# A state-space convolution with a gated MLP: all side jobs of the kernel generation get new places, and the ring buffers new letters

## The chip, the cores and the metric

One core of a Trainium2 chip. The metric is the device time of one execution in microseconds, median of three runs.

## What is computed

`A_u` (called x below) is 2048 positions of 640 channels. A vector `c` gives six modulation rows (scale, shift and gate, twice) by one product with `w_mod`. The first half is a state-space convolution with 192 complex states for each channel: a kernel of 2048 taps is generated and convolved with the modulated input. The second half is a bilinear gated MLP of width 1536. Cut to what matters:

```python
mod = (silu(c) @ w_mod).reshape(1, 6, 1, 640)
sa, ca, ga, sb, cb, gb = mod rows
h = layernorm(x) * (1 + ca) + sa
logdA = exp(log_dt)[:, None] * (A_re + 1j * A_im)
K = einsum("dn,dnl,dn->dl", C, exp(logdA[:, :, None] * l), dt * B).real
y = irfft(rfft(pad(h)) * rfft(pad(K)))[..., :2048] + h * Dskip
x = x + ga * y
h = layernorm(x) * (1 + cb) + sb
out = x + gb * (((h @ w_gate) * (h @ w_up)) @ w_down)
```

## The kernel before

**Kernel generation.** The 640 channels are five groups of 128 (`db` 0 to 4), each generated in eight blocks, 40 blocks (`NK`) in all. The loop at L1325 takes three steps `t` for a block `n`. In a block POOL makes three outer products (`outer`, L716): phases `Pha` or `Phb` (int32), then `EQ`, then `EP`, for the block that follows. ACT takes sines and absolute values of the phases (`tra`, `trb`, `ab`, all through the helper at L230). DVE multiplies them by EQ and EP (`QtA` and `QtB` L771 and L772, `PtA` L777, `PtB` L797). PE contracts the results over the states into a PSUM tile `kg` (L812, L827), and ACT copies it out as `Kt`. EQ and EP have two buffers each, so an EQ can be made only when the QtB two blocks back has read its buffer. For each group the tables of these products come from *seeds* (`u_seeds`): a chain over DVE (to L625), ACT (exponentials, an arctangent), PE (L532 to L534) and DVE (L650, L651). Its last results release POOL's L656, which is followed by the integer tables LH (L699 to L701, L680) and the float table LQ (L710, L711, L680). After the 40 blocks the loop goes on for 24 steps; then comes the GLU.

**Side jobs.** Everything else of the first half runs beside the blocks as generators, each cut into a few parts: `mod_l` loads the modulation weights from `w_mod` (L356), `u_modr` makes a row of the modulation from them (L363) and ACT copies it (tiles TVa, TVb); `u_stats` loads x (L471) and takes its statistics, `u_hm` normalises it on ACT (128 x 640 activations on tiles gha, ghb, f16a and others); `u_k` is the first transform stage of the kernel (L849 on PE, a copy f16b or f16a on ACT); `u_pre` the forward transform of the input (L861 to L884); `u_g` loads a quarter of its spectrum (L910) and carries out the second stage (L894), whose result ACT copies; `u_c` multiplies the spectra (L894 on PE, L935 to L940 on DVE), goes back one stage (L950), copies W on ACT and stores it to DRAM (L955); `u_d` loads it again with x (L963, L965), finishes on PE (L971), adds on DVE (L975 or L978) and stores the row (L979). For the MLP raw weights are loaded (L1004) and split in two parts (`split_g`, L1026), and the *head* normalises the first rows (L1139 and on, L1171, L1206 on PE).

**What sets the order.** Scheduling is manual: each engine carries out its instructions in the order in which the Python code emits them. Nearly all DMAs are issued by SP, in that order too, so a DMA that waits holds back those behind it. A table `SCHED` has for each part of each job a number. `at` files a generator under `v // 10`, a half-step of the loop, and `due` runs those of a half-step in the order of their numbers, so the numbers decide both where a part stands among the blocks and which job comes first. Negative numbers place a part in the seeds of group 0, ahead of the loop. Which letter of a ring of buffers an allocation gets (three PSUM banks `psf`, two each of `TV`, `W`, `tr`, `xs`, three of `gh` and `hf`) stands in the strings of `SLOT`, one letter for each allocation in order of emission; a letter given again is a wait for the tile's former readers.

```python
def at(ts, g, *a):
    it = g(*a)
    for v in ts:
        jobs.setdefault(v // 10, []).append((v, it))
def due(x):
    for _, g in sorted(jobs.pop(x, []), key=lambda j: j[0]):
        next(g, None)
```

## Time and profile before

| | us |
|---|---|
| median of 3 runs | 981.17 (979.21 to 988.58) |
| the profiled execution, its own time | 987.31 |
| its span in the profile | 985.5 |
| PE busy | 892.4 (91%) |
| DVE busy | 717.3 (73%) |
| ACT busy | 579.4 (59%) |
| POOL busy | 513.1 (52%) |
| mean granted TensorE clock | 0.955 |

The shares are means over two halves with different limits: kernel generation to about 437 us, a tail to about 527 us, and the GLU from there. So the prediction reads stretches apart. A row of the timeline is: start, duration, engine, line, operation, output <- inputs, shapes, count, and in brackets the idle time ahead of it with what ended it. A tile's name is cut to its letters (gha, ghb and ghc are one ring).

### The profile page before, as it was taken

How to read it: one execution, taken by the hardware profiler on the slowest of the kernel's cores; microseconds unless marked ns; L12 is line 12 of the kernel's file. 1: busy time of each engine (PE TensorE's matmuls, PEld its weight loads, DVE VectorE, ACT ScalarE, POOL GpSimd, SP SyncE). 2: the span in 40 equal slices, each digit the busy share in tenths (PEclk: the TensorE clock that was granted, in tenths of full speed). 3: DMA queues.
4: the chain of work that ended last, by engine and by line, in shares of the span. 5: the costliest groups of instructions: out<-in, count | busy, mean ns of one | idle time of the engine just before them, and what ended most of it. 6: DMA issues, size and time to landing. Idle time of an engine off the chain costs nothing.

```text
span 985.5 us, 26662 instructions
## 1 busy us (share of the span) xinstructions
PE 892.4 (91%) x11134; PEld 725.6 (74%) x11134; DVE 717.3 (73%) x1297; ACT 579.4 (59%) x1076; POOL 513.1 (52%) x400
## 2 busy tenths in 40 slices
PE   4767898899789888999879999999999999999998
PEld 3565656686476667677636888889999788888997
DVE  8798569888978888794867755557676656578952
ACT  4869989986878797873336433334455443435430
POOL 5988899799779979970030254440113132322110
PEclk9977789899989889999999999999999999999999
DMA  7746664555255434658695666733564576758875
GB/s 260 257 151 212 213 198 137 175 174 173 77 154 175 146 114 116 192 166 269 208 257 189 230 202 188 240 110 132 176 224 129 192 234 220 233 168 293 243 239 187
DMA packets 158816, 188.53 MB, mean 191 GB/s; under 512 B 9828, under 2 KB 128360, under 8 KB 157544
## 3 DMA queue, kind: packets, MB, share of 16 engines
q1 hardware_dynamic: 149480, 155.51, 49.1%
q0 software_dynamic: 4752, 21.63, 7.6%
q10 hardware_dynamic: 4464, 9.70, 2.6%
q8 instruction: 87, 1.43, 0.6%
q14 instruction: 33, 0.27, 0.1%
HBM read 124.22 MB, written 62.59 MB: 190 GB/s over the span
## 4 chain that ended last, share of the span: by engine, by line
PE 56%; ACT 14%; DVE 13%; issue 10%; POOL 4%; DMA 3%; SPq 0%; POOLq 0%; ACTq 0%; DVEq 0%
PE pa L1078 18%; PE psg L1078 9%; PE pa L1502 7%; PE kg L812 2%; PE kg L827 2%; PE psfc L894 2%; PE psfb L894 2%; PE psfc L950 2%; ACT trb L230 2%; ACT L230 2%; PE psfa L894 1%; ACT tra L230 1%; DVE QtA L772 1%; DVE QtA L771 1%; PE psfc L873 1%
## 5 line engine op out<-in xcount | busy, mean ns | idle before, releaser
L1055 POOL TENSOR_TENSOR tf<-wur,wgb 128x256 f32<-128x256 f32 x23 | 17.4, 755 | 243.0 <-DVE wtl L1026 196.5
L716 POOL TENSOR_TENSOR EQ<-LQ,RH 128x1536 f32<-128x1536 f32 x40 | 124.2, 3106 | 8.3 <-DVE QtB L772 8.1
L1026 DVE TENSOR_TENSOR wtl<-tf,wth 128x256 fp32r<-128x256 f32 (+1 forms) x72 | 37.3, 520 | 58.6 <-ACT wth L230 58.4
L716 POOL TENSOR_TENSOR Phb<-LH,DH 128x1536 int32<-128x1536 int32 x20 | 62.3, 3114 | 13.2 <-ACT tra L230 13.2
L716 POOL TENSOR_TENSOR EP<-LP,RH 128x768 f32<-128x768 f32 x40 | 66.1, 1653 | 0.0
L716 POOL TENSOR_TENSOR Pha<-LH,DH 128x1536 int32<-128x1536 int32 (+1 forms) x21 | 62.5, 2974 | 1.9 <-ACT trb L230 1.6
L1502 PE MATMUL pa<-wsg,sh 128*128 128x384 f32 (+1 forms) x304 | 57.3, 307 | 0.0
L827 PE MATMUL kg<-QtB,PtB 64*32 64x64 f32 x2560 | 49.3, 232 | 7.1 <-DVE QtB L772 7.1
L827 PEld LDWEIGHTS kg<-QtB,PtB 64*32 64x32 f32 x2560 | 42.8, 117 | 17.1 <-DVE QtB L772 8.5
L1541 POOL DMA_DIRECT2D wsg<-wdc x21 | 11.1, 531 | 66.5 <-PE pa L1554 35.5
L1502 PEld LDWEIGHTS pa<-wsg,sh 128*128 128x128 f32 x304 | 45.1, 188 | 0.0
L1026 DVE TENSOR_TENSOR wsg<-wga,wsg 128x640 fp32r<-128x640 f32 x36 | 33.8, 946 | 13.2 <-ACT wsg L230 13.2
L230 ACT ACTIVATE sh<-a 128x512 fp32r<-128x512 f32 x55 | 33.3, 624 | 13.9 <-PE psg L1554 6.2
L1026 DVE TENSOR_TENSOR sl<-a,sh 128x512 fp32r<-128x512 f32 x55 | 38.0, 710 | 3.9 <-ACT sh L230 3.9
L230 ACT ACTIVATE wsg<-wga 128x640 fp32r<-128x640 f32 x36 | 26.1, 730 | 24.8 <-PE pa L1502 12.1
L1078 PE MATMUL pa<-hh,wsg 128*128 128x512 f32 x150 | 39.9, 392 | 0.0
L771 DVE TENSOR_TENSOR QtA<-tra,EQ 128x1024 f32<-128x1024 f32 x20 | 24.4, 1221 | 18.1 <-PE kg L812 8.7
L1148 POOL TENSOR_SCALAR hfa<-xb,hr,hr 128x128 f32<-128x128 f32 x4 | 2.3, 577 | 67.0 <-DVE hr L285 67.0
L230 ACT ACTIVATE s<-pa 128x512 f32<-128x512 f32 x12 | 7.2, 599 | 49.1 <-PE pa L1078 49.1
L230 ACT ACTIVATE a<-pa 128x512 f32<-128x512 f32 x12 | 7.2, 597 | 48.4 <-PE pa L1078 48.4
L230 ACT ACTIVATE wth<-tf 128x256 fp32r<-128x256 f32 (+1 forms) x72 | 32.5, 482 | 4.6 <-DVE tf L1056 1.8
L1078 PE MATMUL pa<-sh,wth 128*128 128x512 f32 x110 | 34.0, 390 | 0.4 <-ACT a L230 0.4
(640 smaller groups left out, 3125.4 us busy)
## 6 DMA issues: line engine op xcount, KB each, us to landing
wsg<-wdc POOLq DMA_DIRECT2D x21, 640.0 KB, 4.8
wgb<-B_w_gate SPq DMA_DIRECT2D x24, 320.0 KB, 4.7
wur<-B_w_up SPq DMA_DIRECT2D x24, 320.0 KB, 5.7
wsd<-wsg SPq DMA_DIRECT2D x12, 640.0 KB, 4.2
wga<-wdg SPq DMA_DIRECT2D x12, 640.0 KB, 4.0
wsg<-wsd POOLq DMA_DIRECT2D x12, 640.0 KB, 4.9
wdc<-xb SPq DMA_DIRECT2D x21, 320.0 KB, 3.4
TVb<-WD SPq DMA_DIRECT2D x22, 256.0 KB, 3.4
```

Of the source, the lines that this page charges most:

```text
L230: return S.activation(o, i, f, **kw)
L716: G.tensor_tensor(o.rearrange("p x (h l) -> p x h l", l=8), lo.unsqueeze(2).to_broadcast([P, rows, nh, 8]), hi.rearrange("p h x -> p x h") ...
L771: return [lambda: V.tensor_tensor(Qt[:, :, :, 0:32], tr[:, :, :, ::-1], e[:, :, 0:32].unsqueeze(1).to_broadcast([P, 2, R, 32]), op=OP.mult ...
L812: PE.matmul(kg[j * 32 : j * 32 + 32, dd, :], PtA[:, c, dl * 4 + j, :], QtA[:, c, dl * 4 + j, :], start=dd == 0 and c == 0, stop=False, til ...
L827: PE.matmul(kg[j * 32 : j * 32 + 32, dd, :], PtB[lo : lo + 64, c, r, :], QtB[lo : lo + 64, c, r, :], start=False, stop=dd == 7 and c == 1, ...
L894: PE.matmul(r[c][par * 64 : par * 64 + 64, i, :], t_tw[:, k0 + k, c, :], src[:, k, :], start=True, stop=True, tile_position=(0, par * 64))
L950: PE.matmul(r[par][:, i], t_ti[lo : lo + 64, qd * 4 + i, c, :], x[lo : lo + 64, c, i, :], start=c == 0, stop=c == 1, tile_position=(lo, 0))
L1026: V.tensor_tensor(lo, v, hi, op=OP.subtract)
L1055: E.tensor_tensor(t[:, 0:2], u[:, 0:2], g[:, 0:2], op=OP.subtract)
L1078: PE.matmul(ps, w[a][:, k], x[b][:, l], start=first and n == 0 and m == 0, stop=n == 2 and m == len(ks) - 1, skip_group_check=True)
L1502: PE.matmul(AC[tb][t][c], x[:, ts], w[:, cs], start=st, stop=f == NF - 1 and n == 2 and (c == 0 or t % 2 == 1))
L1541: G.dma_start(WD[q], wdc[:, q // 3, q % 3])
```

## The change

All numbers of `SCHED` are new, and all strings of `SLOT` but `Ph`, `PtA`, `tr` and `f16` (which move in the listing only). No other code differs; the two tables take five more lines, so what was L716 is L721 in the changed kernel, and so on. Each engine has the same instructions in the same numbers; their order differs. A few lines of the tables:

```diff
 SCHED = dict(
-    ml=(-885, -929, -989),
-    mr=(((98, 154), (90, 130)), ((-884, 78), (-877, 73)), ((-885, -881), (-889, 132))),
+    ml=(-880, -916, -945),
+    mr=(((84, 129), (83, 116)), ((-876, 68), (-865, 68)), ((-884, -866), (-881, 7))),
...
-        (338, 577, 594, 672, 676, 688, 718, 745, 812, 816, 825, 855, 872, 872),
+        (500, 538, 549, 670, 678, 691, 732, 742, 805, 811, 826, 845, 859, 866),
...
-        ((2816, 2835, 2861), (2847, 2876, 2876), (2862, 2877, 2878), (2876, 2879, 2879)),
+        ((2776, 2797, 2829), (2804, 2829, 2837), (2780, 2819, 2834), (2844, 2871, 2873)),
...
-    low=((145, 411, 641, 885, 1122, 1398, 1592, 1847, 2073), (209, 434, 680, 929, 1150, 1398, 1612, 1868, 2112)),
+    low=((157, 412, 659, 886, 1134, 1375, 1599, 1842, 2071), (199, 425, 699, 916, 1176, 1367, 1611, 1845, 2116)),
...
-        ((2376, 2550, 2610), (2354, 2464, 2495), (2390, 2442, 2446), (2382, 2455, 2492)),
+        ((2420, 2582, 2583), (2433, 2488, 2511), (2342, 2445, 2481), (2424, 2465, 2485)),
...
 SLOT = dict(
-    gh="abcaacbabcbcbcbacbacabccabcacbabcabc",
+    gh="abcbbcaacacaacabbacbbcaacbacbacbacab",
```

(`ml`, `mr`: the modulation's loads and rows; the third is the seeds of group 1; then `d` of group 4; `low`: LH and LQ tables, first the row for `tab_ph`, then for `tab_eq`; then `g` of group 4.)

Three places show what this does. The first is the start, on SP: loads of x (L471) around the first load of modulation weights, before and then now.

```order
L471 DMA gha<-A_u 128x640
L471 DMA ghb<-A_u 128x640
L356 DMA t_tw<-w_mod 128x5x640
L471 DMA f16a<-A_u 128x640
L471 DMA Wa<-A_u 128x640
L471 DMA ghc<-A_u 128x640
```

```order
L476 DMA gha<-A_u 128x640
L476 DMA f16a<-A_u 128x640 x3
L476 DMA ghb<-A_u 128x640
L476 DMA f16a<-A_u 128x640
L361 DMA t_tw<-w_mod 128x5x640
L476 DMA ghc<-A_u 128x640
```

Two loads of x stood ahead of the weights, and six do now. On PE, the same place: the first modulation rows, behind the seeds' last products. Before, then now:

```order
L534 MATMUL tra<-ct,pta 64x8x8
L363 MATMUL psfb<-t_tw,sil 128x256 x5
L363 MATMUL psfa<-t_tw,sil 128x384 x5
L363 MATMUL psfa<-t_ti,sil 128x384 x5
L363 MATMUL psfc<-t_ti,sil 128x256 x5
```

```order
L539 MATMUL tra<-ct,pta 64x8x8
L368 MATMUL psfb<-t_tw,sil 128x384 x5
L368 MATMUL psfa<-t_tw,sil 128x256 x5
L368 MATMUL psfc<-t_ti,sil 128x384 x5
L368 MATMUL psfb<-t_ti,sil 128x256 x5
```

The 384 wide group of each pair has gone ahead of the 256 wide one (the third and fourth row already stood so). ACT's copy of the 384 wide row stands ahead of the first sines, as before; the copy of the other one stands behind the first pair of them.

The second place is DVE at the end of block 5, with the seeds of group 1. Before, from block 5's PtB on:

```order
L797 TENSOR_TENSOR PtB<-tra,EP_145 128x512
L771 TENSOR_TENSOR QtB<-tra,EQ_143 128x16x32
L772 TENSOR_TENSOR QtB<-tra,EQ_143 128x16x32
L595 TENSOR_TENSOR RL_158<-psfa,mults 128x288
L597 TENSOR_TENSOR RH_154<-psfa,mults 128x1056
L458 COPY colT<-psfb 128x5
L607 TENSOR_SCALAR psfc<-ptb 128x192
L620 SCALAR_TENSOR_TENSOR prm<-ptb,dt_100,psfc 128x192
L621 SCALAR_TENSOR_TENSOR psfc<-psfc,ptb 128x192
L622 RECIPROCAL psfc<-psfc 128x192
L623 SCALAR_TENSOR_TENSOR pta<-pta,psfc 128x192
L624 TENSOR_TENSOR psfc<-pta,psfc 128x192
```

Now:

```order
L600 TENSOR_TENSOR RL_158<-psfc,mults 128x288
L602 TENSOR_TENSOR RH_154<-psfc,mults 128x1056
L612 TENSOR_SCALAR psfb<-ptb 128x192
L625 SCALAR_TENSOR_TENSOR prm<-ptb,dt_100,psfb 128x192
L626 SCALAR_TENSOR_TENSOR psfb<-psfb,ptb 128x192
L627 RECIPROCAL psfb<-psfb 128x192
L628 SCALAR_TENSOR_TENSOR pta<-pta,psfb 128x192
L629 TENSOR_TENSOR psfb<-pta,psfb 128x192
L630 TENSOR_SCALAR pta<-psfb 128x192
L802 TENSOR_TENSOR PtB<-tra,EP_145 128x512
L776 TENSOR_TENSOR QtB<-tra,EQ_143 128x16x32
L777 TENSOR_TENSOR QtB<-tra,EQ_143 128x16x32
```

The run of seed instructions stood behind the block's QtB and stands ahead of it now. On ACT the part from there to the arctangent has six normalisations where it had eight, and on POOL the add at L865 has moved ahead of the EQ of that block.

The third place is POOL at the tables of group 3, behind the seeds' last part. Before, from the second pair of L655 and L656 on:

```order
L655 TENSOR_TENSOR ptb<-ptb,DL_163 128x96
L656 TENSOR_TENSOR DL_163<-ptb 128x4x24
L699 TENSOR_TENSOR DH_159<-DH_159 128x192
L700 TENSOR_TENSOR LH<-DL_162,eighth 128x192
L701 TENSOR_TENSOR LH<-LH,DL_162 128x192
L680 TENSOR_TENSOR LH<-LH,DL_162 128x192x2
L680 TENSOR_TENSOR LH<-LH,DL_162 128x192x4
L710 COPY LQ<-RL_157 128x96
L711 TENSOR_TENSOR LQ<-RL_157 128x96
L680 TENSOR_TENSOR LQ<-LQ,RL_157 128x96x2
L680 TENSOR_TENSOR LQ<-LQ,RL_157 128x96x4
L716 TENSOR_TENSOR Pha<-LH,DH_159 128x1536
```

Now, from the product ahead of them on:

```order
L721 TENSOR_TENSOR EP_145<-LP_149,RH_156 128x768
L715 COPY LQ<-RL_157 128x96
L716 TENSOR_TENSOR LQ<-RL_157 128x96
L685 TENSOR_TENSOR LQ<-LQ,RL_157 128x96x2
L685 TENSOR_TENSOR LQ<-LQ,RL_157 128x96x4
L660 TENSOR_TENSOR ptb<-ptb,DL_162 128x96
L661 TENSOR_TENSOR DL_162<-ptb 128x4x24
L660 TENSOR_TENSOR ptb<-ptb,DL_163 128x96
L661 TENSOR_TENSOR DL_163<-ptb 128x4x24
L704 TENSOR_TENSOR DH_159<-DH_159 128x192
L705 TENSOR_TENSOR LH<-DL_162,eighth 128x192
L706 TENSOR_TENSOR LH<-LH,DL_162 128x192
```

The four instructions that make LQ have moved from behind the LH tables to ahead of L655.

In the tail, on SP, the four loads of the last group's spectrum (L910) stood in a row between the last two WD stores of group 3 (L955); now one stands ahead of both and three behind both, and the last store's number is lower (2394 for 2412). The three loads of group 4's rows (L963) stand ahead of a raw weight load (L1004) that stood ahead of them. On PE two groups of L971 stood behind the last gate product of the head (L1206); now the last L971 stands ahead of its last two pairs, and three second-stage groups on f16b (L894) have moved behind the last L827.

191 lines of the change are left out of this document (99 added, 92 removed), and 41 rows, old and new, of tables (c, d, g, pre).

## The prediction

> **What bounds the kernel now.** I read the table of engines by stretches first, cut at 25 us (the first outer products), where POOL's last outer product ends (437.5 us) and where the GLU starts (527 us). Columns: window and its length, busy time of each engine with its instructions, granted TensorE clock, DMA share, GB/s.
>
> ```profile
> 25.00:437.50 412.50, 353.11 (x7630) 262.49 (x7630) 340.39 (x523) 344.48 (x630) 373.38 (x222) 0.90 0.53 166
> 437.50:527.00 89.50, 74.98 (x1073) 54.22 (x1070) 57.00 (x140) 34.34 (x62) 9.36 (x15) 0.98 0.76 235
> 527.00:985.50 458.50, 453.19 (x2401) 401.07 (x2399) 298.65 (x545) 188.57 (x362) 116.87 (x138) 1.00 0.62 202
> ```
>
> In the last stretch PE is busy for 453 of 458 us, and the change leaves the GLU's order alone, so I take 458.5 us there as fixed. In the long stretch POOL has 373 of 412 us, the most of any engine, but ACT (344) and DVE (340) are close: an interlock with POOL ahead. The next view is what POOL waits for there (waits summed, times, longest).
>
> ```profile
> POOL Phb L716 <- ACT tra L230: 13.2, 4, 6.7
> POOL DL L656 <- issue: 10.6, 2, 7.9
> POOL EQ L716 <- DVE QtB L772: 8.1, 3, 5.0
> ```
>
> These 31.9 us, with 2.6 in two shorter rows, are all that a better order can win in that stretch as long as POOL's work is the same. It is: every engine carries out the same instructions before and after, and only their order and the buffers' letters differ. The rest is the tail, 89.5 us, in which POOL has nothing to do and PE is busy for 75.
>
> **The start.** The first trigonometric block can't begin until ACT has copied a modulation row that PE makes from w_mod.
>
> ```profile
> 8.98 0.43 SPq L356 DMA_DIRECT2D t_tw<-w_mod  x1
> t_tw<-w_mod SPq DMA_DIRECT2D x1, 1600.0 KB, 8.3
> 12.00:18.60 6.60, 2.28 (x12) 1.59 (x12) 6.36 (x15) 5.40 (x14) 6.21 (x9) 1.00 0.96 370
> 18.67 4.64 PE L363 MATMUL psfb<-t_tw,sil 128*128 128x256 f32 x10
> 23.09 3.69 PE L363 MATMUL psfa<-t_tw,sil 128*128 128x384 f32 x10
> 26.82 0.48 ACT L230 ACTIVATE TVa<-psfa 1x384 f32<-1x384 f32 x1 [9.34 <-PE psfa L363]
> ```
>
> Before, ACT waits for the second group of ten matmuls, the 384 wide one, behind the 256 wide one. Now the 384 wide one comes first, and the other row's copy is behind the first pair of activations. A price for the wide group at this place isn't in the trace. From below it is its 3.69 us; from above the first group's 4.64 scaled by the width, x 1.5 = 7.0. The 256 wide group took longer than the wider one behind it, so part of the 4.64 belongs to the place and not to the width: I take 5.4, about halfway.
>
> Against it, four more loads of x, 320 KB each, stand ahead of the weights in SP's queue. At the 370 GB/s of that window they are 1.31 MB / 370 = 3.5 us. The weights landed at 8.98 + 8.3 = 17.3, PE took them at 18.67, so 1.4 us are free and the delay lies between 0 (the loads that stood behind the weights shared the engines with them, so only their order changes) and 2.1 us; I take 1.0, halfway. So the copy starts at 18.67 + 1.0 + 5.4 = 25.1 in place of 26.82: **1.7 us gained**, between 4.4 gained (18.67 + 3.69 = 22.4) and 0.9 lost (18.67 + 2.1 + 7.0 = 27.8).
>
> The Trainium skill, DMA: Bandwidth & Descriptors, section "Queues, rings and completion order", says that descriptors of one queue are taken by each engine in ring order. By that rule the whole 2.1 us is lost and the start gains 0.7 in place of 1.7; no row here shows a load of that size behind six others, so the trace can't decide it. The same skill, TensorE: Matmul & The Clock Gate, Part 1, says that the first 3.4 us or so of sustained matmuls run at half rate whatever they are; this speaks against the lower bound of 3.69. The granted clock of the window up to 18.60 reads 1.00, so no row here shows it.
>
> **From 75 to 119 us.** The next place where an order was changed and POOL waits is the seeds of group 1. They are a chain over DVE, ACT (an arctangent) and PE, whose end releases the tables on POOL.
>
> ```profile
> 92.68 3.09 POOL L716 TENSOR_TENSOR EQ<-LQ,RH 128x1536 f32<-128x1536 f32 x1
> 98.35 1.26 POOL L865 TENSOR_TENSOR hfa<-hfa,f16a 128x512 f32<-128x512 f32 x1 [0.97 <-DMA hfa<-hm]
> 102.61 0.38 POOL L656 TENSOR_TENSOR DL<-ptb 128x96 int32<-128x96 int32 x1 [2.65 <-issue]
> 113.50 3.10 POOL L716 TENSOR_TENSOR EQ<-LQ,RH 128x1536 f32<-128x1536 f32 x1
> ...
> 74.54:92.32 17.78, 13.57 (x222) 10.07 (x222) 16.03 (x29) 17.53 (x30) 15.19 (x6) 0.80 0.46 155
> ...
> 91.64 0.68 DVE L772 TENSOR_TENSOR QtB<-tra,EQ 128x512 f32<-128x512 f32 x1
> 92.24 0.45 DVE L595 TENSOR_TENSOR RL<-psfa,mults 128x288 f32<-128x288 f32 x1
> 97.25 0.36 DVE L625 TENSOR_SCALAR pta<-psfc 128x192 f32<-128x192 f32 x1
> 112.23 0.68 DVE L772 TENSOR_TENSOR QtB<-trb,EQ 128x512 f32<-128x512 f32 x1
> ...
> 100.12 0.36 ACT L230 ACTIVATE pta<-pta 128x192 f32<-128x192 f32 x1
> 104.38 0.91 ACT L230 ACTIVATE ghb<-ghb,nm,rs 128x640 f32<-128x640 f32 x1
> ```
>
> ACT carried out eight normalisations of x (tiles ghb and the like, 0.91 us each) between the block before and the arctangent at 100.12; now six, and one 512 wide copy of a spectrum that lay in a wait before (by the rate of the 0.91, 512/640 of it, less some overlap: 0.6). That is 2 x 0.91 - 0.6 = 1.2 us off the chain, after which one more normalisation (0.9) stands ahead of the next QtB's inputs.
>
> DVE pays for it. The run from L595 (92.24) to the end of L625 (97.61), 5.37 us, stood behind block 5's QtB and stands ahead of it now; DVE's idle time in blocks 4 and 5, 17.78 - 16.03 = 1.75 us of that window, can take up as much. QtB(5) ends at 92.32 + 5.37 - 1.75 - 1.7 = 94.2, and EQ, which takes its buffer over, starts there and not at 92.68. POOL uses that wait, since the 1.26 us at L865 has moved ahead of EQ; EQ and EP took from 92.68 to 98.35 - 0.97 = 97.38, so EP now ends near 94.2 + 4.7 = 98.9. The seeds end at 102.61 - 1.7 - 1.2 = 99.7. So the tables come 2.9 us earlier; but the EQ at 113.50 starts only when QtB at 112.23 is through, and that row follows ACT: 1.7 + 1.2 - 0.9 = **2.0 us earlier**. What the start gains is in this number, not to be added to it. From block 10 to 22 the same instructions stand in the same blocks, so the 2.0 travel on. Bounds: 4.4 + 0.3 = 4.7 gained with the best start; 0.9 - 0.3 = 0.6 lost with the worst.
>
> **Near 270 us.** The seeds of group 3 hold POOL for 7.91 us, and behind them stand first the integer tables, then LQ, then the next Pha.
>
> ```profile
> 277.18 0.39 POOL L656 TENSOR_TENSOR DL<-ptb 128x96 int32<-128x96 int32 x1 [7.91 <-issue]
> 282.80 0.37 POOL L710 COPY LQ<-RL 128x96 f32<-128x96 f32 x1
> 284.98 3.12 POOL L716 TENSOR_TENSOR Pha<-LH,DH 128x1536 int32<-128x1536 int32 x1
> 295.78 3.10 POOL L716 TENSOR_TENSOR EQ<-LQ,RH 128x1536 f32<-128x1536 f32 x1
> ...
> 289.84 0.41 DVE L554 TENSOR_SCALAR psfc<-pta,dt 128x192 f32<-128x192 f32 x1
> 293.69 0.68 DVE L772 TENSOR_TENSOR QtB<-tra,EQ 128x512 f32<-128x512 f32 x1
> ```
>
> The four LQ instructions take 284.98 - 282.80 = 2.18 us and need no seed of the chain; the new order puts them ahead of L656, into the wait. Pha then starts 2.2 us earlier. The next thing that can hold POOL is the EQ at 295.78, whose buffer is free at 294.37: 1.4 us of room, and some 1.6 more because four small DVE instructions (the first at 289.84, 0.41 us) ahead of that QtB move a block later. I take **2.0 us**, between 2.2 and 0 (the chain over PE is what the block waits for in the end).
>
> **The tail.** After 437 us the last group's convolution and the head of the GLU are one chain over DVE, DMA and PE.
>
> ```profile
> 439.80 0.33 SPq L955 DMA_DIRECT2D WD<-Wa  x1
> 441.13 2.36 SPq L910 DMA_DIRECT2D f16a<-FH  x4
> 448.16 0.32 SPq L955 DMA_DIRECT2D WD<-Wb  x1
> 453.48 1.15 PE L894 MATMUL psfb<-f16b,t_tw 128*64 128x64 f32 x32
> 458.40 0.69 DVE L935 TENSOR_TENSOR TVb<-psfc,f16a 128x512 f32<-128x512 f32 x1 [9.59 <-ACT f16a L230]
> ...
> 492.85 0.37 SPq L1004
> 493.85 5.28 DMA TVa<-WD
> 521.17 0.99 PE psfb L971 x8
> 523.08 0.70 DVE xsa L978
> ```
>
> Three edits: the two last L971 groups with their sums (521.17 to 523.78, 2.6 us behind the last gate matmul) move ahead of the last head matmuls, which then carry two adds of 0.7: 1.5 gained. The load at 493.39 leaves its place behind a raw weight load (492.85, waited for DVE); the WD store it needs lands at about the same moment, so 0.5. Three of the four spectrum loads of 441.13 move from between the last two WD stores of group 3 to behind the last (448.16), which gives issues near 448.5 and landings, by the 5.28 of the row below it, near 453.8; PE used their data from 453.48 + 1.15 = 454.6 on, so they land just in time. Some of PE's groups on f16b (1.15 each) move behind the last kg group, which delays the first of f16a and speeds up the kg group by as much. I take 0 for both, with the loss priced below as a rival. Sum of the tail **2.0 us**, between 5.2 gained (the closing 2.6 in full, and half of the 5.28 load) and 4.6 lost (four f16b groups of 1.15).
>
> **The sum.** 2.0 + 2.0 + 2.0 = 6.0 us against the profiled execution's 987.31 (its span of 985.5 and 1.8 around it): 981.3. That execution lay 6.1 above the median of the runs, 981.17, so on the median's basis I forecast **975.2 us**. Its own range from the bounds: 4.7 + 2.2 + 5.2 = 12.1 gained to 0.6 + 4.6 = 5.2 lost, 969.1 to 986.4.
>
> **Rivals.** No change: POOL's long waits for ACT (the 6.7 among the 13.2) lie behind the blocks with seeds of a later group, whose ACT instructions are the same in number and kind as before; if those blocks are paced by ACT alone, what is gained ahead of them is swallowed, and only about 1 us of the tail is left: 980. For it: the waits are long. Against it: ACT itself waits for POOL's products between them, so a shift travels through.
>
> Faster: the copies behind the small spectrum matmuls hold ACT.
>
> ```profile
> ACT f16a L230 <- PE psfa L849: 8.3, 3, 6.2
> ACT f16b L230 <- PE psfa L849: 6.6, 3, 3.0
> ```
>
> Of the 40 such copies, nine stood in the same half-step as their matmuls and two do now. If ACT so loses most of these 14.9 us in places that POOL waits on, half of POOL's 34.5 (31.9 and 2.6) goes: 981.2 - 17.2 = 964. Against it: ACT is not the busiest engine of the stretch, and a wait of ACT that POOL does not feel costs nothing.
>
> Slower: the three spectrum loads in the tail. One mechanism: in SP's queue they now stand behind the last WD store of group 3, and a store waits for ACT's copy of a PE result. The last two stores came 8.4 us apart (439.80 to 448.16). If the last one comes one such step behind 448.16, since its PE groups have new neighbours too, the loads are issued at 456.6 and land, by the 5.28 of the nearest row, at 461.9 against a use at 454.6: 7.3 lost, and 3 x 1.15 = 3.4 more as three f16b groups ahead of them have moved behind the last kg group: 10.7 us, 992. It decides from the point where that store is issued after about 449 (454.6 - 5.3). Against it: the store's own place has moved ahead by nearly two half-steps.
>
> **How the numbers follow.** Forecast 0.42, no change 0.17, faster rival 0.25, slower rival 0.16. A measurement of this kernel tells about 1% from no change, that is 971.4 and 991.0. Faster by over 1%: the faster rival and a small part of the forecast's lower end, 0.28. Slower: the slower rival, whose price has no cap, and starts that lose in more places than I priced, 0.18. Within 1%: 0.54. The range for 8 in 10, from just below the faster rival's time to just past the slower one's: 962 to 993.
>
> **What would show it.** Right: first QtA near 28.7 in place of 30.45; the 2.65 gap at L656 near 100 smaller than 1 and EQ at about 111.5; a 7.9 gap near 268 with the LQ rows inside it or ahead of it; POOL's last product near 433.5; the last L971 ahead of the last L1206 and the first GLU matmul (526.68) near 520.7. Wrong: a DVE wait for f16a above 9.6 us in the tail (slower rival), POOL waits for ACT that stay at 13.2 while the start is earlier and the end of POOL is not (no change), or waits below 17 us in all (faster rival).

## The result: slower by 0.6%, and the profile after

| | before | changed |
|---|---|---|
| median of 20 runs each, us | 982.29 (979.21 to 988.58) | 989.06 (983.26 to 994.34) |
| ratio to before, 95% interval | | 1.0058 (1.0038 to 1.0079) |
| the profiled execution, its span, us | 987.31, 985.5 | 984.10, 982.3 |

By the ratio the change costs 5.7 us. One thing must be known before the profiles are compared: the profiled execution of the kernel before lies near the top of its spread and that of the changed kernel near the bottom of its own, so these two profiles alone show the wrong sign. So I profiled both kernels once more (980.1 and 983.16 us), and I use stretches and several profiles, not one pair of spans. Five single executions of the kernels compared here took 1042 us or more, and the ratios leave them out.

The table engines by stretches of the changed kernel, cut at the same three events as before (start of the products, POOL's last outer product, first GLU matmul):

```profile
25.00:441.00 416.00, 347.78 (x7644) 254.85 (x7642) 340.11 (x524) 343.80 (x629) 373.42 (x222) 0.91 0.52 163
441.00:521.40 80.40, 69.82 (x1045) 51.12 (x1046) 57.63 (x141) 32.43 (x59) 6.81 (x13) 1.00 0.86 258
521.40:982.30 460.90, 455.51 (x2419) 403.38 (x2417) 298.52 (x545) 191.16 (x365) 119.03 (x141) 1.00 0.62 203
```

The long stretch has grown (412.5 to 416.0, against an unusually long one before), the tail has shrunk (the same event to the same event: 86.6 to 80.3), the GLU is as long as it was. POOL's waits in the long stretch (line, what it waited for, us in all, times, longest):

```profile
POOL Phb L721 <- ACT tra L235: 15.9, 3, 7.8
POOL EQ L721 <- DVE QtB L777: 11.0, 4, 5.0
POOL LQ L715 <- DVE RL L655: 7.3, 1, 7.3
```

34.2 us in three rows, where before there were 31.9; over all rows 37.8 against 34.5, and in the second pair of profiles 38.5 against 30.0. The sum has risen, and where L656 stood, LQ stands.

Where the loss is made can be read from the end of POOL's last product (EP, L716, now L721) of a block; the first product of the GLU is L1169 on xb, 523.8 us before (my forecast's 526.68 is a later row). The means are over four profiles of the old order (the two, the table alone at 604, the kernel before with the changed tail) and five of the changed one (the two, and the experiments on u_d(1,1), on the start and on LQ); the last row leaves out the one with the changed tail. The experiments that move the table into or out of the critical place are not in the means.

| us, end of | before, two profiles | changed, two profiles | mean before | mean changed | made in the stretch |
|---|---|---|---|---|---|
| block 8 | 118.2, 118.3 | 117.5, 117.6 | 118.2 | 117.6 | -0.6 |
| block 15 | 188.6, 188.5 | 195.0, 193.1 | 188.3 | 195.0 | +7.3 |
| block 23 | 268.9, 267.7 | 273.3, 271.4 | 268.1 | 273.6 | -1.1 |
| block 31 | 360.4, 356.2 | 364.2, 364.7 | 356.9 | 365.4 | +2.9 |
| block 39, the last | 437.3, 433.1 | 441.1, 441.6 | 433.8 | 442.7 | +0.4 |
| from there to the first GLU matmul | 86.6, 84.0 | 80.3, 78.5 | 85.1 | 80.5 | -4.6 |

The sum is +4.2, inside the 3.7 to 7.8 us of the ratio's interval. Three stretches matter: **blocks 9 to 15 lose 7, blocks 24 to 31 lose 3, the tail gains 4.6**. In my forecast only the third existed. The 7 us are made in two steps. Block 9 takes 12.4 to 13.0 us in the five changed profiles and 10.2 in all four old ones; block 15 takes 16.3 to 18.6 against 12.6 to 13.3. POOL's wait in block 15, before and changed:

```profile
179.86 3.11 POOL L716 TENSOR_TENSOR Phb<-LH,DH 128x1536 int32<-128x1536 int32 x1 [4.65 <-ACT tra L230]
185.09 3.12 POOL L721 TENSOR_TENSOR Phb<-LH,DH 128x1536 int32<-128x1536 int32 x1 [7.77 <-ACT tra L235]
```

**Block 15.** It begins 40 us earlier, at the table load. In the changed kernel, SP's issues, then the landings of the same window (KB each, us from issue to landing; the third row is the same kind of store in the second profile of the kernel before), then what ACT and PE wait for:

```profile
139.07 0.50 SPq L1255 DMA_DIRECT2D t_tw<-t_tw  x1
145.40 0.37 SPq L886 DMA_DIRECT2D FH<-hfb  x1
145.89 1.48 SPq L889 DMA_DIRECT2D FH<-hfa  x2
```

```profile
t_tw<-t_tw SPq DMA_DIRECT2D x1, 2048.0 KB, 11.4
FH<-hfb SPq DMA_DIRECT2D x1, 256.0 KB, 7.1
FH<-hfc SPq DMA_DIRECT2D x1, 256.0 KB, 3.5
```

```profile
153.31 0.60 ACT L235 ACTIVATE hfa<-psfa 128x512 f32<-128x512 f32 x1 [4.86 <-DMA FH<-hfa]
154.44 1.98 PE L854 MATMUL psfc<-ct,Kta 128*64 128x128 f32 x16 [4.26 <-ACT hfc L235]
```

```profile
152.00:156.00 4.00, 1.56 (x16) 1.56 (x16) 1.00 (x4) 2.66 (x6) 3.92 (x4) 0.52 0.42 111
```

The table t_tw (2 MB) now goes out at number 604 in place of 487. It keeps the DMA engines busy until 150.5, and in that time SP issues the stores of FH. A store that nobody reads for a while looks harmless, but the buffers hfa and hfb are free only when it has landed, and that of hfb takes 7.1 us. ACT's next copy into hfa waits 4.9 us for hfa's store, issued right behind hfb's; PE waits 4.3 behind ACT, and when PE comes back its granted clock is 0.52. POOL runs ahead and is the last to feel it, in block 15. Block 9 ends at 130, before the table is issued, so its 2.5 us have another cause: there Phb waits 1.7 us for ACT's tra and the add L870 0.8 us for a load of hfb, and the kernel before has neither wait. What put them there was not tried.

**Blocks 24 to 31.** ACT's copy of ghc and, behind it, DVE:

```profile
301.40 0.60 ACT L235 ACTIVATE ghc<-psfa 128x512 f32<-128x512 f32 x1 [3.57 <-PE psfa L899]
```

```profile
304.65 0.69 DVE L802 TENSOR_TENSOR PtB<-trb,EP 128x512 f32<-128x512 f32 x1 [4.05 <-ACT trb L235]
```

The copy of u_g(2,2) stands one half-step behind its matmuls (1460, 1470), where it stood three half-steps behind (1413, 1449). ACT reaches it before PE is through (1.2 us of its 3.6 are a gap of PE inside that very group of matmuls), and the copies trb and tra of the sines, which DVE needs, are queued behind it. POOL feels it late here too: in these two kernels' profiles its blocks 24 and 25 are as long as ever, and the wait comes in block 31, whose ACT work is full. In the second profile of the kernel before, then in the changed kernel:

```profile
348.41 3.12 POOL L716 TENSOR_TENSOR Phb<-LH,DH 128x1536 int32<-128x1536 int32 x1 [3.58 <-ACT tra L230]
356.43 3.11 POOL L721 TENSOR_TENSOR Phb<-LH,DH 128x1536 int32<-128x1536 int32 x1 [6.39 <-ACT tra L235]
```

One profile does not decide this stretch: in the first profile of the kernel before the same wait is 6.75.

### The profile page after: what moved, and what is told of

Read it like the earlier page. It is cut to its first block, busy times and chain, and to the rows that moved or that the text cites. A ratio compares the mean times of both kernels' runs of the same rounds, so it can differ in the third digit from the quotient of the medians.

```text
span 982.3 us, 26647 instructions
## 1 busy us (share of the span) xinstructions
PE 882.0 (90%) x11134; PEld 714.8 (73%) x11134; DVE 717.3 (73%) x1297; ACT 579.4 (59%) x1076; POOL 512.9 (52%) x400
## 4 chain that ended last, share of the span: by engine, by line
PE 52%; ACT 14%; DVE 11%; issue 10%; DMA 7%; POOL 5%; SPq 1%; POOLq 0%; DVEq 0%; ACTq 0%
PE pa L1083 18%; PE psg L1083 9%; PE pa L1507 7%; ACT trb L235 2%; PE psfb L899 2%; PE psfa L899 2%; PE psfc L899 2%; ACT tra L235 2%; PE kg L832 1%; ACT L235 1%; PE kg L817 1%; DMA hfc<-hm 1%; POOL EQ L721 1%; PE psfa L955 1%; DMA t_tw<-w_mod 1%
## 5 line engine op out<-in xcount | busy, mean ns | idle before, releaser
L721 POOL TENSOR_TENSOR EQ<-LQ,RH 128x1536 f32<-128x1536 f32 x40 | 124.0, 3101 | 11.1 <-DVE QtB L777 11.0
L721 POOL TENSOR_TENSOR Phb<-LH,DH 128x1536 int32<-128x1536 int32 x20 | 62.2, 3111 | 16.0 <-ACT tra L235 15.9
L721 POOL TENSOR_TENSOR EP<-LP,RH 128x768 f32<-128x768 f32 x40 | 65.9, 1648 | 0.0
L721 POOL TENSOR_TENSOR Pha<-LH,DH 128x1536 int32<-128x1536 int32 (+1 forms) x21 | 62.4, 2971 | 2.8 <-ACT trb L235 2.4
L832 PE MATMUL kg<-QtB,PtB 64*32 64x64 f32 x2560 | 46.8, 224 | 10.6 <-DVE QtB L777 7.4
L832 PEld LDWEIGHTS kg<-QtB,PtB 64*32 64x32 f32 x2560 | 39.8, 111 | 18.3 <-issue 8.9
L1031 DVE TENSOR_TENSOR wsg<-wga,wsg 128x640 fp32r<-128x640 f32 x36 | 33.9, 946 | 13.3 <-ACT wsg L235 13.3
L235 ACT ACTIVATE sh<-a 128x512 fp32r<-128x512 f32 x55 | 33.3, 624 | 13.9 <-PE psg L1559 6.2
L235 ACT ACTIVATE wsg<-wga 128x640 fp32r<-128x640 f32 x36 | 26.2, 730 | 23.5 <-PE pa L1507 11.9
```

Of the source, the lines that this page charges most:

```text
L235: return S.activation(o, i, f, **kw)
L721: G.tensor_tensor(o.rearrange("p x (h l) -> p x h l", l=8), lo.unsqueeze(2).to_broadcast([P, rows, nh, 8]), hi.rearrange("p h x -> p x h") ...
L832: PE.matmul(kg[j * 32 : j * 32 + 32, dd, :], PtB[lo : lo + 64, c, r, :], QtB[lo : lo + 64, c, r, :], start=False, stop=dd == 7 and c == 1, ...
L1031: V.tensor_tensor(lo, v, hi, op=OP.subtract)
```

## The experiments

All ratios are to the kernel before, from runs on the same chip.

**The table's place, tried in both kernels.** The changed kernel with the table load back, and the kernel before with the new place:

```diff
-    tab=(604, 753),
+    tab=(487, 753),
```

> The changed kernel with one number put back: the load of the 2 MB transform table (tables, t_tw) at half-step 48 in place of 60, as before the change. Theory (the table load fills the DMA engines just when stores must land that free the transform's buffers): the ACT wait of 4.9 us for FH<-hfa near 148 us falls under 1 us, block 13's ACT end moves from 185 back to about 180.5, and the time falls by 3 to 6 us, to about 984 to 986. Rival (the order of the blocks 9 to 13 on ACT and DVE themselves): no change, 989. Second rival (the letters of the buffer ring: any store is late there): the wait stays at 3 us or more.

> The kernel before with that one number of the change alone: the 2 MB table load at half-step 60 in place of 48. Theory: ACT's 0.6 us wait for a store near 149 us grows to 3 to 6 us and the time rises by 3 to 6 us, to about 985 to 988. Rival (other edits of the change are needed for the loss, the buffers' letters or the order of the stores): within 1 us of the kernel before, 982.

Measured: 1.0025 (1.0003 to 1.0047) and 0.9999 (0.9976 to 1.0022). Going back wins some 3 us by the ratios, whose intervals overlap, but block 15 ends at 197.9 in its profile, later than in the changed kernel: block 15 itself is down to 14.4 us, and block 11 is up from 9.1 to 14.5. The new place costs the kernel before nothing. So "the table came too early" or "too late" is no cause. Both profiles say why. In the changed kernel with the table at 487, the six loads of the seeds of group 2 stand right behind it (their first number was changed from 338 to 500; my words behind the diff of the change call this row group 1 by mistake):

```profile
122.60 1.24 SPq L1255 DMA_DIRECT2D t_tw<-t_tw  x1
127.38 0.48 SPq L554 DMA_DIRECT2D pta<-A_A_im  x1
```

```profile
134.44 0.46 ACT L235 ACTIVATE prm<-pta,dt 128x192 f32<-128x192 f32 x1 [6.09 <-DMA pta<-A_A_re]
```

In the kernel before with the table at 604, nothing in front of it in SP's queue had to wait, so SP issued the load at 134.41, and the next FH store comes 10.8 us later and lands in 2.7:

```profile
134.41 1.38 SPq L1250 DMA_DIRECT2D t_tw<-t_tw  x1
145.17 0.36 SPq L881 DMA_DIRECT2D FH<-hfc  x1
```

The two unedited kernels, profiled again beside these:

> The kernel before once more, unchanged, for a second profile: the first profiled execution (987.31) lay at the upper end of its runs (979 to 989, median 982.3), that of the change (984.10) at the lower end of its own (983 to 994, median 989.1), so a comparison of those two profiles alone shows the wrong sign. If the spread sits in one place (a wait for a DMA that comes or does not come), this profile differs from the first by several us there and is the same to 0.5 us elsewhere; if it is spread over the whole, block ends drift apart gradually.

> The changed kernel once more, unchanged, for a second profile. Theory: the change lost its time near 148 us, where ACT waits 4.9 us for a store of a transform buffer to land while a 2 MB table load is under way; that wait comes again here (3 to 8 us), and POOL's last product ends 3 to 10 us after that of the kernel before (437.3). Rival: the loss is elsewhere and this profile has no such wait.

Measured: 980.1 and 983.16, one execution each; the table of block ends above holds both. Their spans differ by 3.1 us, within what single executions differ, and so decide nothing. The wait for FH<-hfa came again (4.0 us), and POOL's last product ends 4.3 us after 437.3, as the theory had it. The spread of the kernel before sits in few places: its two executions agree to 0.2 us up to block 22, and their 7.2 us come from block 23 (1.3), block 31 (3.1) and the tail (2.6). Ahead of that block 31, from 322 to 326 us, the granted clock reads 0.50 in the slower one and 1.00 in the other.

**The collision, put into the kernel before.** If the theory is right, the table right ahead of those stores must hurt there too:

```diff
-    tab=(487, 829),
+    tab=(640, 829),
```

> The kernel before with one number changed: the 2 MB load of the twiddle table from 487 to 640, which puts it behind the load of hfb and the store of gbd and right ahead of the three FH stores at 145 us in SP's queue; nothing else moves. Theory (a collision of the table with those stores is enough to make the loss of the blocks 10 to 15): the FH stores land in 5.5 to 8 us instead of 2 to 3, ACT's copy hfa or hfc behind them waits 3 to 6 us, PE stands as long and resumes at about half the granted clock, POOL's block 15 ends at 191.5 to 195 instead of 187.4 to 188.6, and the time is 3 to 6 us above the kernel before (ratio 1.003 to 1.006). Rival (the loss needs the changed kernel's other places as well: the seed loads, the earlier hm stores and the gh buffers): block 15 ends below 190, ratio 0.998 to 1.002.

Measured: 1.0050 (1.0033 to 1.0068), block 15 at 193.1 in place of 188.3.

```profile
141.96 0.43 SPq L1250 DMA_DIRECT2D t_tw<-t_tw  x1
146.12 0.37 SPq L881 DMA_DIRECT2D FH<-hfc  x1
...
152.93 0.60 ACT L230 ACTIVATE hfc<-psfc 128x512 f32<-128x512 f32 x1 [3.27 <-DMA FH<-hfc]
```

```profile
t_tw<-t_tw SPq DMA_DIRECT2D x1, 2048.0 KB, 10.1
FH<-hfc SPq DMA_DIRECT2D x1, 256.0 KB, 6.7
```

One load moved, no other engine's order touched, and the same wait appears. PE waits 2.9 us behind it, and its granted clock reads 0.65 from 156 to 160. Block 15 takes 17.6 us, as in the changed kernel, and blocks 9 and 11 are as before: the collision by itself is enough for the loss of block 15, 4 to 5 of the 7 us.

**The collision, taken out of the changed kernel.** First with the seeds' loads put back ahead of the table:

```diff
-    tab=(604, 753),
+    tab=(487, 753),
...
-        (500, 538, 549, 670, 678, 691, 732, 742, 805, 811, 826, 845, 859, 866),
+        (338, 538, 549, 670, 678, 691, 732, 742, 805, 811, 826, 845, 859, 866),
```

> The changed kernel with the 2 MB twiddle table back at number 487 AND the first loads of the third seed group (ptb and pta from A_B, A_C, A_A) back at number 338, so that these six loads stand ahead of the table in SP's queue again, as they did before the change; the other engines' orders are the changed kernel's. Theory (a bulk load of about 11 us must have nothing behind it in the queue that somebody waits for): neither the wait of ACT for pta (6.1 us near 134 us) nor that of ACT for the stores of FH (4.9 us near 153 us) is there; POOL's block 15 ends at 188 to 190 us (before 188.2 to 188.6, changed 192.9 to 194.8, table alone moved 197.6), its last product ends at 435 to 437.5, and the time comes to 984 to 985.5 us where the kernel before stands at 982.3 (ratio 1.001 to 1.003). Rival (the blocks 10 to 15 are full, and a wait taken away comes back as another one in the next block): block 15 ends above 192, the last product above 440, ratio 1.005 or more.

Measured: 1.0095 (1.0068 to 1.0122), a clear miss. The wait for pta is gone, but SP, which issues in order, stands 12.3 us at the first of the six loads, whose buffer is not free, and what is queued behind comes late: hfa's load is issued at 122.27 in place of 117.27, and POOL waits for it.

```profile
103.02 0.33 SPq L552 DMA_DIRECT2D ptb<-A_B_re  x1
127.85 1.26 POOL L870 TENSOR_TENSOR hfa<-hfa,f16a 128x512 f32<-128x512 f32 x1 [5.21 <-DMA hfa<-hm]
```

The table itself goes out at 126.65, behind that load, so this loss is not the collision and says nothing for or against it; what failed is my claim that the old pair of places would suit the new order. The changed order has no gap of 11 us between 120 and 150 at all. So I cut the load in quarters: two at 604, one at 665, one at 760.

```diff
-        SY.dma_start(t_tw.rearrange("p b r m -> p (b r m)"), I["t_tw"])
+        for q in qs:
+            SY.dma_start(t_tw[:, 8 * q : 8 * q + 8].rearrange("p b r m -> p (b r m)"), I["t_tw"][:, 1024 * q : 1024 * q + 1024])
...
-    at(T0["tab"][:1], once(tables))
+    for v, qs in ((604, (0, 3)), (665, (1,)), (760, (2,))):
+        at((v,), once(tables), *qs)
```

> The changed kernel with the 2 MB load of the twiddle table cut in quarters: two quarters (the ones that the first L899 groups read) stay at number 604, the third goes to 665, behind the FH stores and the loads of gh, and the fourth to 760; nothing else moves. Theory (the table, 11 us of all DMA engines, lies right ahead of the FH stores at 145 us, which free hfa and hfb): with 1 MB at that place it lands by about 145, the FH stores land in 3 us instead of 5.7 to 7.1, ACT's 4.0 to 5.1 us wait for hfa near 153 us is under 1, POOL's block 15 ends at 188.5 to 190.5 instead of 192.9 to 195.8, its last product at 437 to 440 instead of 440.9 to 444.1, and the time is 4 to 5.5 us below the changed kernel (ratio to the kernel before 1.000 to 1.002). Rival (loss of the blocks 10 to 15 lies in the side jobs' engine work there, not in the table): the wait goes, block 15 still ends at 193 or later, ratio 1.005 or more.

Measured: 1.0020 (0.9995 to 1.0045), 3.8 us better than the changed kernel by the ratios, whose intervals just overlap. ACT's wait for hfa fell from 4.9 to 2.3, not under 1, and block 15 ends at 191.9, not 190.5: about half of the stretch's loss is back. Where the half is can be read from the blocks: block 15 takes 13.9 us, near the 12.6 to 13.3 of the old order, while block 9 still takes 12.7 and block 11 9.9, against 10.2 and 9.0. The rest is not this collision.

**Blocks 24 to 31.** The loads of u_d(1,1) had been put behind three FH stores, and PE's L976 stood for them:

```diff
-        ((1529, 1579, 1580), (1570, 1593, 1627), (1946, 2030, 2038), (1616, 1714, 1740)),
+        ((1529, 1579, 1580), (1546, 1593, 1627), (1946, 2030, 2038), (1616, 1714, 1740)),
```

> The changed kernel with one number changed: the loads of u_d(1,1) (TVa from WD, xsb from A_u) back from 1570 to 1546, so that they stand ahead of the three FH stores at 1565 in SP's queue instead of behind them; nothing else moves. Theory (the loads stood behind stores that wait for ACT's copies, and PE's in-order queue then stood at L976): the wait of PE's L976 for TVa near 321 us (3.1 us) is gone, ACT's trb copy near 324 comes 2 to 3 us earlier, POOL's block 31 ends at 361 to 362 instead of 364.1 to 364.5, and the time falls by 2 to 3 us (ratio to the kernel before 1.002 to 1.004). Rival (ACT's copy hfc near 328 needs L878 of the same stretch, and POOL is paced by the whole block's ACT work): the wait at L976 goes, block 31 still ends at 364, ratio 1.005 to 1.007.

Measured: 1.0058 (1.0036 to 1.0079): nothing, though the wait at L976 is gone as both said. Block 31 ends at 367.5. The wait for ghc is the largest again, now 6.0:

```profile
ACT ghc L235 <- PE psfa L899: 6.0, 1, 6.0
```

So its rival was right about the time: L976 is no cause that the times show. Then the other place, with it and alone (the edit also exchanges four letters of `psf`, which follow from the new order of allocation):

```diff
-        ((1403, 1841, 1870), (1259, 1513, 1521), (1280, 1460, 1470), (1679, 1778, 1783)),
+        ((1403, 1841, 1870), (1259, 1513, 1521), (1280, 1413, 1449), (1679, 1778, 1783)),
```

> The changed kernel with two numbers changed: the loads of u_d(1,1) back to 1546 as in the run that did that alone, and the matmuls and copies of u_g(2,2) back from 1460 and 1470 to 1413 and 1449, as before the change. Theory (the loss of the blocks 24 to 31, about 3 us from POOL's block 23 to its block 31, comes from these two places: ACT's copy of ghc that waits 3.6 to 6.0 us for L899 of the same half-step, and PE's L976 that stood behind a late load): the ghc wait near 300 us falls below 2 us, POOL's blocks 23 to 31 take 88 to 89.5 us (before 87.6 to 88.5 in three runs of four, changed 90.9 to 93.3), and the time is 2 to 3.5 us below the changed kernel (ratio 1.002 to 1.004). Rival (PE is full in these blocks, and the earlier L899 only moves its time ahead of L976 and L817): POOL's blocks 23 to 31 still take 91 us or more, ratio 1.005 to 1.007.

> The changed kernel with one job changed: the matmuls and copies of u_g(2,2) back from 1460 and 1470 to 1413 and 1449, so that ACT's copy of ghc no longer stands one half-step behind its matmuls and ahead of the tra and trb copies. Theory A (this copy alone held ACT, PE and DVE near 300 us; the late load of u_d(1,1) lay beside other waits): ratio 1.001 to 1.004, as with both edits. Theory B (both were needed): ratio 1.004 to 1.007, and PE's L976 near 320 us still waits 2 to 3 us for the load of TVa. In both the ghc wait near 300 us is below 2 us.

Measured: both 1.0021 (1.0002 to 1.0040), u_g(2,2) alone 1.0007 (0.9993 to 1.0022). Alone it wins all that the pair wins, with PE still waiting at L976:

```profile
PE psfc L976 <- DMA TVa<-WD: 2.8, 1, 2.8
```

So the place of u_g(2,2) is the edit that counts, with its matmuls, copy and letters together. The profiles agree: from the end of block 23 to that of block 31 this run takes 89.0 us, the changed kernel 90.9 and 93.3. Over all profiles on record the nine with the old place take 87.6 to 91.5 us, 89.3 in the mean, and the eight with the new one 90.9 to 93.3, 91.9 in the mean. In the profile of the run with both edits they take 91.3, outside what I expected, and there a likely cause can be seen. PE in it, from u_pre (L878) behind a wait to the next L899; and the same instructions in the run with all edits below:

```profile
323.00 1.22 PE L878 MATMUL psfb<-hfa,ct 64*64 64x512 f32 x2 [1.59 <-issue]
327.43 1.93 PE L832 MATMUL kg<-QtB,PtB 64*32 64x64 f32 x64
331.86 0.44 PE L899 MATMUL psfa<-f16b,t_tw 128*64 128x128 f32 x4
```

```profile
318.70 1.04 PE L878 MATMUL psfb<-hfa,ct 64*64 64x512 f32 x2 [1.59 <-issue]
321.37 1.10 PE L832 MATMUL kg<-QtB,PtB 64*32 64x64 f32 x64
324.81 0.44 PE L899 MATMUL psfa<-f16b,t_tw 128*64 128x128 f32 x4
```

Equal instructions behind an equal wait of 1.59 us: 8.9 us here, 6.1 there. The granted clock is the difference, 0.50 from 326 to 330 in the first and 1.00 in the second:

```profile
326.00:330.00 4.00, 4.00 (x78) 2.40 (x72) 3.29 (x3) 2.99 (x6) 3.92 (x3) 0.50 0.43 131
```

```profile
318.00:322.00 4.00, 3.30 (x60) 1.26 (x64) 4.00 (x8) 0.94 (x2) 3.92 (x5) 1.00 0.79 227
```

**All three edits together.**

> The changed kernel with both edits together: the twiddle table in quarters (604, 665, 760), and u_d(1,1) and u_g(2,2) back. Theory (the two losses are separate and add up, and the tail's gain of 4 to 5 us is left): POOL's last product at 433.5 to 437, 79 to 82 us from there to the first GLU matmul, time 976 to 981 us where the kernel before stands at 982 to 983 (ratio 0.994 to 0.998). Rival (one loss hides the other, or comes back elsewhere): ratio 1.000 or more.

Measured: 0.9979 (0.9954 to 1.0004), 979.8 us. 1.0058 less the 0.0038 of the quarters and the 0.0037 of the two numbers is 0.9983: within the intervals, the losses are separate and add up. POOL's last product ends at 435.0, the tail takes 79.3, and block 23 to 31 take 88.4 in its profile.

**The tail alone, and the early part alone.** Two kernels cut together from both tables: the kernel before with the changed tail, and the changed places below number 900 with the old ones behind (buffers of the second part handed out anew in both). The first, cut to two rows; the others are `k` from 35 on, `wl`, `wm`, `c` and `g` of group 4, and the rows of `c` and `d` that begin above 2330:

```diff
-    w=(2508, 2575, 2790, 2776, 2819, 2829),
+    w=(2545, 2570, 2737, 2815, 2806, 2768),
-    h=(2480, 2716, 2875, 2876, 2878, 2878, 2878, 2878),
+    h=(2570, 2762, 2831, 2851, 2852, 2852, 2870, 2877),
...
```

> The kernel before with only the tail of the change: the numbers of all side jobs from about half-step 233 on (the last block's g, c and d jobs, the last five u_k, the raw weight loads, warm and the head) are those of the change, and the buffers from there on are handed out as in the change; everything up to POOL's last products is the kernel before. Theory (the tail's gain belongs to the tail's own places): POOL's last product ends where it did (431 to 437), the first GLU matmul comes 79 to 81 us after it instead of 84 to 87, and the time falls by 4 to 6 us (ratio 0.994 to 0.996, about 977 us). Rival (the tail only looked short because POOL came late, and work that doesn't depend on POOL had piled up ready by then): 84 us or more from the last product to the first GLU matmul, ratio 0.999 to 1.001.

> A kernel cut together from both: all side jobs that begin below number 900 (the start, the stages up to POOL's block 15) at the places of the change, all later ones at the places of the kernel before, buffers from number 900 on handed out after the order of the kernel before. Theory (the loss is made in the first 195 us, and the later places give and take little but for the tail): POOL's block 15 ends at 192.5 to 196, the blocks 23 to 31 take 87.5 to 89 us, POOL's last product comes at 437.5 to 440.5, the first GLU matmul 84 to 87 us after it, and the time is 4 to 7 us above the kernel before (ratio 1.004 to 1.008). Rival (the blocks up to 15 differ in the two profiles, but POOL makes up for it later in the old places): last product at 434 or earlier, ratio 1.000 to 1.002.

Measured: 0.9964 (0.9946 to 0.9983) and 1.0086 (1.0054 to 1.0119). The tail alone, 80.6 us from a last product at 433.2, wins 3.5 us (expected 4 to 6); this has the lowest median found, 978.8 us, faster than both kernels, though its interval overlaps that of all three edits. The early part alone costs the whole loss and more: block 15 at 196.8, the last product at 444.5 (expected 437.5 to 440.5), 86.9 us from there to the GLU. Its blocks 23 to 31 take 90.2 us (expected 87.5 to 89), so part of what is lost there does not need u_g(2,2).

**The start.** The weights' load ahead of five of the six loads of x again:

```diff
-    ml=(-880, -916, -945),
+    ml=(-880, -916, -996),
```

> The changed kernel with one number changed: the load of the first modulation weights from -945 to -996, so that only one x load stands ahead of it in SP's queue instead of six; nothing else moves. Theory of the start in the forecast (the 384-wide group first gains if its weights are there in time): PE's first L368 group no longer waits 2.2 us for t_tw, starts near 18.8 us, ACT's first TVa copy comes at 24.7 instead of 26.88, the first QtA at 28.3 instead of 30.5, and the time falls by 1.5 to 2.2 us (ratio to the kernel before about 1.004). Rival (POOL's block 1 and 2 end at 35.7 and 43.4 us whatever the first QtA does, and the six x loads that come later are waited for by the row statistics): the wait goes, yet the time stays at ratio 1.005 to 1.007, or another wait shows up in the first 120 us.

Measured: 1.0042 (1.0020 to 1.0065), which the times can't tell from the changed kernel. The trace can. The wait is gone and ACT's copy comes at 24.71, 2.2 us ahead:

```profile
18.76 5.91 PE L368 MATMUL psfb<-t_tw,sil 128*128 128x384 f32 x10
```

```profile
24.71 0.48 ACT L235 ACTIVATE TVa<-psfb 1x384 f32<-1x384 f32 x1 [7.14 <-PE psfb L368]
```

The first QtA comes at 29.16, not at 28.3, since it now waits for POOL's EQ, and by 70 us nothing of the lead is left. The expectation's rival shows in the trace: a load of x that now stands behind the weights holds DVE for 0.85 us, the seeds of group 0 end later, and POOL begins its products at 24.43 in place of 23.36.

```profile
19.71 0.89 DVE L484 BATCH_NORM_STATS2 st<-ghb 128x6 f32<-128x320 f32 x2 [0.85 <-DMA ghb<-A_u]
```

Then DVE is held in the row statistics, in an instruction on 128 x 6 elements that takes 0.17 us elsewhere, until a product of POOL is through (67.41 + 3.10 = 70.51, 67.50 + 3.03 = 70.53; in the changed kernel both end at 69.5):

```profile
67.50 3.03 DVE L287 TENSOR_TENSOR ry<-ry,rv 128x6 f32<-128x6 f32 x1
```

```profile
67.41 3.10 POOL L721 TENSOR_TENSOR Phb<-LH,DH 128x1536 int32<-128x1536 int32 x1
```

The QtB behind it ends at 74.5, in the changed kernel at 74.4. Nothing of the 2.2 us travels on.

**LQ ahead of L661.**

```diff
-    low=((157, 412, 659, 886, 1134, 1375, 1599, 1842, 2071), (199, 425, 699, 916, 1176, 1367, 1611, 1845, 2116)),
+    low=((157, 412, 659, 886, 1134, 1375, 1599, 1842, 2071), (199, 425, 699, 916, 1176, 1398, 1611, 1845, 2116)),
```

> The changed kernel with one number changed: the last LQ products of POOL (2.2 us) back from 1367 to 1398, behind the L660 and L661 products of the next seeds, as before the change. Theory (LQ reads RL, which the end of the seeds writes, so that ahead of L661 it waits for the same event, and nothing is won or lost): POOL's wait of 7.2 to 7.5 us for RL turns into one of 8 us ahead of L661, block 23 ends within 1 us of the changed kernel's (counted from the end of block 22), ratio 1.004 to 1.007. Rival (the forecast's step: 2 us are won by having LQ done in the gap): POOL's block 23 takes 2 us longer, ratio 1.007 to 1.009.

Measured: 1.0036 (1.0015 to 1.0058), not to be told from the changed kernel. The LQ rows lie in block 24, not in block 23 as I expected; it takes 23.3 us here, 23.5 and 23.4 in the two profiles of the changed kernel. The wait has only changed its name:

```profile
POOL DL L661 <- issue: 7.3, 1, 7.3
```

## Why the prediction was wrong, point by point

**The sign.** I forecast 975.2; the median is 989.06. I priced four places where an order that POOL waits on had changed, and took everything else as moved within slack: "from block 10 to 22 the same instructions stand in the same blocks, so the 2.0 travel on". That step failed, and its premise was misread: with 60 numbers of `SCHED` to a block, 43 of the 152 numbers that place a part in blocks 10 to 22, in one kernel or the other, place it in another block than before, and the table load is one of them (block 8 before, 10 now). What the runs showed in its place: in block 15, 4 to 5 us by the table's load against the FH stores; in blocks 24 to 31, 3 us, with the place of u_g(2,2) as the edit that counts; and in block 9, 2.5 us whose cause stays open. The lead of each part over the part it needs was in the tables, and I counted it for the u_k copies only. A rival of the right kind was there (stores in SP's queue, 10.7 us), in the wrong place. That the time still lies in my range of 962 to 993 is luck: its upper end came from that rival.

**Start, 1.7 gained: 0.** Two estimates failed. The 384 wide group took 5.93, not 5.4, and the weights came late by the whole 2.2 us, not by 1.0.

```profile
20.92 5.93 PE L368 MATMUL psfb<-t_tw,sil 128*128 128x384 f32 x10 [2.21 <-DMA t_tw<-w_mod]
```

```profile
26.88 0.48 ACT L235 ACTIVATE TVa<-psfb 1x384 f32<-1x384 f32 x1 [9.44 <-PE psfb L368]
```

26.88 in place of 26.82. The Trainium skill, DMA: Bandwidth & Descriptors, section "Queues, rings and completion order", had been weighed for this: one queue's descriptors are taken in ring order, so all bytes ahead count. The trace agrees (2.2 late against the 2.1 worked out by that rule), and I should have taken it in place of the middle. But the larger error is in the sum: the run with the weights in time shows that its gain at the start does not reach 75 us.

**75 to 119 us, 2.0 gained: 0.6, and lost again in block 9.** POOL in the changed kernel:

```profile
96.60 3.09 POOL L721 TENSOR_TENSOR EQ<-LQ,RH 128x1536 f32<-128x1536 f32 x1 [2.75 <-DVE QtB L777]
...
101.71 0.39 POOL L661 TENSOR_TENSOR DL<-ptb 128x96 int32<-128x96 int32 x1
...
112.81 3.10 POOL L721 TENSOR_TENSOR EQ<-LQ,RH 128x1536 f32<-128x1536 f32 x1
...
119.21 3.12 POOL L721 TENSOR_TENSOR Phb<-LH,DH 128x1536 int32<-128x1536 int32 x1 [1.69 <-ACT tra L235]
```

The mechanism is as worked out: EQ waits for QtB(5), the gap at L661 is gone, the next EQ is earlier. The sizes are not: EQ came at 96.60, where I had 94.2, 1.7 of it because the gain of the start was in it, and 112.81 where I had 111.5. Right behind, Phb waits 1.7 us for ACT's tra, which itself had to wait for DVE to be through with that buffer (QtA, L777), and block 9 ends 2.0 later than before. The term was right up to its last row and I had stopped reading there.

**Near 270 us, 2.0 gained: 0.** "Need no seed of the chain" was wrong. LQ reads RL, and DVE writes RL in L655, among the last results of that chain:

```profile
280.62 0.36 POOL L715 COPY LQ<-RL 128x96 f32<-128x96 f32 x1 [7.32 <-DVE RL L655]
```

The row that should have told me lies in the trace of before (DVE L650 writes RL as the seeds end). A product moved into a wait gains only if its inputs are there before the wait ends.

**Tail, 2.0 gained: 4.6, and 3.5 by itself.** The direction held, the main term was taken too small. The last L971 groups with their sums, 2.6 us behind the last gate matmul before, are gone from the end in full; I had taken 1.5. In the kernel before with this tail PE goes from the last gate matmul straight to the GLU:

```profile
513.53 0.39 PE L1206 MATMUL psg<-hl,wsg 128*128 128x512 f32 x1
513.77 1.47 PE L1169 MATMUL pa<-ident,xb 128*128 128x128 f32 x12
```

The rest, 0.9 to 2 us, lies ahead of that matmul; which of the other edits made it was not tried apart. The slower rival came, but small. In the changed kernel the longest wait of DVE in the tail is 5.3 us, but a sum of L983 with a wait of 5.1 stands just ahead of it; in the kernel before with this tail the wait of that product is 10.6, above my 9.6. The product starts 21.6 to 22.8 us behind POOL's last one in the three profiles of the changed kernel and of this one, 21.1 and 19.4 in the two before: 1 to 3 us late, not 10.7, and the tail makes them up.

**The GLU, fixed: right.** 461.4 us in the mean of three and of five profiles.

**No change, and the faster rival.** The u_k copies that left their matmul's half-step (ten stood there by the tables, not nine) freed ACT, as the rival said: its waits for L849, now L854, into f16a and f16b fall from 20.7 to 15.5 us. But POOL's waits rose from 34.5 to 37.8 us, so this won nothing that could be seen.

## What to carry to other kernels

A bulk load has a length in time, here 8 to 11 us for 2 MB, and the stores issued within that length landed after 5.4 to 7.1 us in place of 2.7 to 3.9; so before such a load is moved, list the transfers behind it in the queue, stores included, since a store's landing is what frees its buffer. List those behind any load that must wait for its own buffer too: one such wait of 12.3 us, in the kernel with the seeds ahead of the table, came with the largest loss among the changed kernel's experiments. In an interlock of three engines look at the distance of every consumer from its producer on an in-order engine (here one half-step cost ACT 3.6 to 6 us, three half-steps at most 0.8), and follow a predicted gain row by row until the block that ends it, since a wait ahead of the next rendezvous eats it. When single executions spread by 1%, compare the same event over several profiles.

## What the runs showed of the hardware

- **The granted clock makes a wait dearer, and not always.** Behind the 4.3 us wait of PE near 154 us the clock reads 0.52 in the changed kernel. Behind a wait of 1.59 us equal matmuls took 8.9 or 6.1 us in two runs (0.50 against 1.00). The Trainium skill, TensorE: Matmul & The Clock Gate, Part 1, speaks of a half-rate state after about 3.4 us idle and of a window that runs freely, so that equal kernels differ; the trace agrees with the second, and the wait of 1.59 us is shorter than the first. Over the four sets of 23 to 27 executions of the kernel before, time and mean granted clock go together (correlation -0.41 to -0.76, 0.2 to 0.5 us for each 0.001); this may be part of the 1% spread, and which of the two drives the other is not shown.
- **Small DVE instructions can last until a product of POOL ends.** The 3.03 us above, and 2.32 us for 128 x 6 elements at the same place of the changed kernel, both end within 0.03 us of POOL's product of 3.1 us. The Trainium skill, GPSIMD Engine Reference, section "Key points", says that the two engines share SBUF interfaces; no run here separates that from another cause.
- **PE stood idle for 1.2 to 2.6 us in the middle of one L899 group**, put down to "issue", near 300 us, in ten profiles of kernels with the changed middle. Whether instructions came late was not tried.
